# Two more Strassen pairs in block 0, and sums made by accumulating transfers

## The chip, the cores and the metric

The kernel runs on one core of a Trainium2 chip. The time is device time of one execution in microseconds; the median of three executions is given, and the profile is of one more execution. Engines are named as in the profile: PE (matrix products), DVE (vector), ACT (activation), POOL (GpSimd), SP (issues transfers). PE's weight loads are shown apart, as PEld.

## The reference

With x = A_u (2048 rows of 640) the result is x plus two branches that both start from a layer norm without scale:

```
xn = (x - mean) / sqrt(var + eps)                    # over the 640 columns
A  = causal convolution of xn with an S4D kernel, plus xn * D_skip
B  = mish(xn @ w1 + b1) @ w2                         # 640 -> 1728 -> 640
return x + A + B
```

Branch B is nearly all the arithmetic. mish(h) is h * tanh(softplus(h)).

## The kernel before

**Tiling.** The 2048 rows are worked in four blocks b of 512. Everything is held transposed: 640 features are five slabs k of 128 partitions, rows are the free dimension. F = 1728 is cut into 14 chunks f (thirteen of 128, and f = 8 of 64). Each fp32 product is three fp16 products (high x high, low x high, high x low), so the weights (W1H, W1L, W2H, W2L) and x (XH, XL) are split into high and low halves: ACT rounds the high half (`hi_w1` L522, `hi_w2` L529, `hi_x` L535), DVE makes the low half.

**A chunk.** The first layer (`mm1`, fifteen matmuls of 512 columns, L773) fills a PSUM bank, which the profile calls h or tr. The mish chain follows on ACT and DVE: sigmoid (L863), product with h (L867), three polynomial steps on ACT (L872, L877, L882), product (L887), rounding (L894) and low half (L905). The second layer (`mm2`, fifteen matmuls, L825) adds into five banks acc; it runs three chunks behind the first.

**Pairs by Strassen's identity.** In blocks 1 to 3 the first layers of the chunk pairs starting at 0, 2, 4, 6, 9, 11 are made together (`mm1_pair`, L775): 54 matmuls of 256 columns (L793) in five parts named one, two, three_a, three_b and four, in place of 60. It needs sums of weights of the two chunks (SWH, SWL, and the unused high half of W1H), sums of x (TH, TL, EH, EL), and between its parts two copies on ACT (cV L1029 and cY L1030, PSUM to a buffer and PSUM to PSUM) and two sums on DVE (z L1033, which part three_a waits for, and w L1037). Second-layer matmuls are woven between the parts. The sums of weights are made once, for block 1: SP loads both chunks again (`load_s`, two whole chunks a pair), DVE makes four sums (`sum_w`), then ACT and DVE round them (`hi_s` L568, `lo_s` L572). Block 0 has only plain chunks.

**The next block's x.** During block b, SP loads the rows of block b + 1 in four tiles for the statistics on DVE (L597 to L599) and the transposed x in five slabs (`load_xt`). POOL makes the inverse deviation (`rstds`), PE transposes mean and deviation into one bank (`spread` L608, after chunk 7 in block 0 and inside the pair at chunk 6 later), ACT copies it (L612), SP stores it to DRAM (sd, L616) and loads it back spread over all partitions (bc, L620, two tiles). DVE subtracts the mean and multiplies (`norm_t` L624, ten instructions a block). ACT and DVE split the result and make the sums of x (`sum_x`, `hi_t`, `lo_t`).

**The rest.** Branch A is reduced to two running sums per slab (`skip_a` to `skip_e`: DVE scans L715 and L719, the result L729 added into the slab xt). At a block's end the acc banks go to buffers r (`join`, L734 on DVE and L736 on ACT), and POOL's transfers do the rest: `add_x` (L518) adds the original x into r, `finish` (L739) adds r into xt, `store` (L742) writes xt out. The first two are accumulating transfers. SP also loads w1 and w2 again, transposed, for a check of their size (L666, L669).

**What sets the order.** The class `Plan` writes the program: each piece of work is added with its engine, a cost, what it needs (pre), the buffer it takes and, for transfers, kilobytes. PE's order is fixed by the code; every other engine takes, by these costs, the piece with the earliest due time among those ready. A transfer is taken to share one line with all others at 300 KB a microsecond, and to land 1.9 us after its bytes; `add_x` and `finish` are charged at twice their bytes, 512 for 256 KB. The result is a fixed order of instructions on each engine; at run time each engine works in that order and waits where it must. POOL and SP issue their transfers in order too. Semaphores of transfers are eight for each of the two queues, used in turn.

Of the kernel before, what the change touches and what calls it, by code (L numbers as in the profile page):

```python
# [20 lines left out]
P = 128  # L21
L = 2048
D = 640
# [10 lines left out]
HALF = 8  # L34
LAG = 3
# [201 lines left out]
def ffn_general(tc, x, xT, vec, w1, w2, out):  # L237
# [3 lines left out]
    with ExitStack() as es:  # L241
# [12 lines left out]
        for b in range(NB):  # L254
# [11 lines left out]
            for f, (n, o) in enumerate(zip(FC, FO)):  # L266
# [5 lines left out]
                for k in range(KD):  # L272
                    pe.matmul(h[:n], W1[:, k, :n], XN[:, k], start=k == 0, stop=k == KD - 1)
# [149 lines left out]
def body(ctx: ExitStack, tc: tile.TileContext, x, xT, logA, Aim, Cr, Ci, logdt, vec, w1, w1T, w2, w2T, out):  # L423
# [64 lines left out]
    XT, ACT, SM, NX = ({} for _ in range(4))  # L488
    NCHK = NF + 3 * KD
# [51 lines left out]
    def load_s(i, j):  # L541
# [3 lines left out]
    def sum_w(i, j):  # L545

        w = lambda n, m: kf(pl["sw", i, n])[:, 0:4].rearrange("p (q j) f -> p q j f", j=2)[:, :, m]
        t = lambda n: pl["ss", i, n // 2].rearrange("p (j q f) -> p j q f", j=2, q=2)[:, n % 2]
        if j == 0:
            v.tensor_tensor(t(0), w(1, 0), w(1, 1), op=OP.add)  # L550
        elif j == 1:
            v.tensor_tensor(t(1), t(0), w(0, 0), op=OP.subtract)
        elif j == 2:
            v.tensor_tensor(t(2), w(0, 0), w(1, 0), op=OP.subtract)
        else:
            v.tensor_tensor(t(3), w(0, 1), t(1), op=OP.subtract)

    def part_w(i, j):
        f = PAIRS[i] + 1
        t = pl["ss", i, j // 2].rearrange("p (j q f) -> p j q f", j=2, q=2)  # L560
        if j == 0:
            sh, sl = (w[f][:, 0:4].rearrange("p (q j) f -> p q j f", j=2)[:, :, 0] for w in (W1H, W1L))
            return sh, sl, t[:, 0]
        return (SWH[i][:, 0], SWL[i][:, 0], t[:, 1]) if j == 1 else (SWH[i][:, 1:3], SWL[i][:, 1:3], t)
# [12 lines left out]
    def sum_x(c, j):  # L577

        x = XT[c][:, 0:4].rearrange("p (q j) t -> p q j t", j=2)
        b11, b12, b21, b22 = (x[:, :, i, h] for i in range(2) for h in (CA, CB))  # L580
        p, q = ((b12, b11), (b22, j == 1 and stage(c, 0)), (b22, b12), (b21, j == 3 and stage(c, 1)),
                (XT[c][:, 4, CA], XT[c][:, 4, CB]))[j]
        v.tensor_tensor(stage(c, j), p, q, op=OP.subtract)

    def hi_t(c, j):
        a.activation(EH if j == 4 else TH[j], stage(c, j), AF.Copy, scale=SX)

    def lo_t(c, j):
        hi, lo = (EH, EL) if j == 4 else (TH[j], TL[j])
        v.scalar_tensor_tensor(lo, stage(c, j), SX, hi, op0=OP.mult, op1=OP.subtract)  # L590
# [27 lines left out]
    def spread_l(c):  # L618
        for j in range(2):
            sp.dma_start(pl["b", c][j], NX["sd"][j * NT:(j + 1) * NT].rearrange("(o i) p -> o (i p)", o=1).to_broadcast([P, TB]))  # L620

    def norm_t(c, k, j):
        z = XT[c][:, k]
        v.tensor_tensor(z, z, pl["b", c][j], op=(OP.subtract, OP.mult)[j])  # L624

# [118 lines left out]
    def bank(b, f):  # L744

        if b > 0:
# [3 lines left out]
    def mm1_part(f, kinds, c, start=False, stop=False, ks=range(KD)):  # L750
# [3 lines left out]
        for j, ((w, x), k) in enumerate(seq):  # L754
            pe.matmul(bank(0, f)[:, c], w[:, k], x[k][:, c], start=start and j == 0, stop=stop and j == len(seq) - 1)  # L755

    def mm1(b, f):
# [3 lines left out]
        hh, lh, hl = ([(h, w[f][:, k], x[k]) for k in range(KD)] for w, x in ((W1H, xh), (W1L, xh), (W1H, xl)))  # L761
# [13 lines left out]
    def mm1_pair(b, f):  # L775

        i = PAIRS.index(f)
        wh = [[W1H[f + j][:, k] for k in range(KD)] for j in range(2)]
        wl = [[W1L[f + j][:, k] for k in range(KD)] for j in range(2)]
# [133 lines left out]
    def whole():  # L913
# [8 lines left out]
        def chain(b, f, pre, drop=()):  # L922
# [7 lines left out]
            elif b > 0 and f in PAIRS:  # L930
# [52 lines left out]
        for f in range(3, NF):  # L983
            prev = {3: 0, 4: 1}.get(f, f - 2)
            add(("m1", 0, f), M, 15 * M5 if FC[f] == P else 1.85, mm1, 0, f,
                pre=[("hw1", f), ("ow1", f), ("v1", 0, prev), ("sg", 0, prev)] if f > 3 else [("v1", 0, prev), ("sg", 0, prev)])
            chain(0, f, [("m1", 0, f)])
            if f == 7:
                add(("spread", 1), M, 0.1, spread, pre=[("rs", 1)])
            for o in second(0, f - LAG, []):  # L990
                o()


        def vc(b):
            return ("vX", b - 1, PAIRS[-1]) if b > 1 else ("v1", 0, 2)

        for b in range(1, NB):
            for f in range(NF):
                n = (b, f)
                if f - 1 in PAIRS:  # L1000
# [3 lines left out]
                if f not in PAIRS:  # L1004
                    pb = before(b, f)
                    add(("m1", *n), M, 15 * M5 if FC[f] == P else 1.85, mm1, b, f,
                        pre=[("v1", b, f - 2), ("sg", b, f - 2)])
                    chain(b, f, [("m1", *n)])
                    for o in second(*g2, []):
# [3 lines left out]
                c = b  # L1013
                one, two, three_a, three_b, four = mm1_pair(b, f)
                p0 = (b, PAIRS[i - 1]) if i else (b - 1, PAIRS[-1])
                first = b == 1 and i == 0
                lastB = ("v1", 0, LAST) if first else ("v1", *before(b, f)) if f in (0, 9) else ("v1", *p0)
                lastC = ("v1", 0, LAST - 1) if first else ("v1", p0[0], p0[1] + 1)
                lastA = [("v1", 0, 2), ("sr", 1)] if first else [("cY", *p0), ("vX", *p0)]
                if (b, i) in ((1, 4), (2, 4), (3, 4)) and b < NB - 1:  # L1020
                    lastA.append(("sr", b + 1))
                if (b, i) == (NB - 1, NP - 1):
                    lastA.append(("oke",))
                SWD = lambda j: [("os", i, j)] if b == 1 else []
                TXD = lambda j: [("tl", b, j)]
                XLD = lambda ks: [("lo", b, k) for k in ks]
                A2, B2 = second(*g2, [9] if FC[g2[1]] == P else [6]), second(*h2, [3, 9] if FC[h2[1]] == P else [2, 6])
                add(("one", *n), M, 12 * M2, one, pre=lastA + SWD(0) + TXD(0) + XLD((0, 2)))
                add(("cV", *n), A, 0.36, lambda: a.copy(PVS, PV), pre=[("one", *n)] + ([] if first else [("w", *p0)]))  # L1029
                add(("cY", *n), A, 0.36, lambda: a.copy(PY, PX), pre=[("cV", *n), lastC])  # L1030
                A2[0]()
                add(("two", *n), M, 15 * M2, two, pre=[("cY", *n)] + SWD(1) + TXD(1) + XLD((1, 3, 4)))
                add(("z", *n), V, 0.38, lambda: v.tensor_tensor(PZ, PY, PVS, op=OP.add), pre=[("two", *n), lastB])  # L1033
# [7 lines left out]
                if i == NP - 2 and b == NB - 1:  # L1041
                    add(("oks",), M, 0.1, ok_sum, pre=[("ce", "last"), ("vX", *n)])
# [7 lines left out]
                chain(b, f + 1, [("four", *n), ("w", *n)])  # L1050

# [30 lines left out]
        for c in range(1, NB):  # L1082
            b = c - 1
            t0 = start(b, 0)
            for i in range(NT):
                add(("lx", c, i), S, 0.1, lambda c=c, i=i: sp.dma_start(pl["x", c, i], xr[c, i]),
                    pre=[("st", c, i - 2)] if i > 1 else [], take=("x", ("x", c, i), 1), rel=t0, kb=327.0)
# [4 lines left out]
            add(("bc", c), S, 0.2, spread_l, c, pre=[("sd", c)], take=("b", ("b", c), 2 * KD), kb=512.0)  # L1092
# [260 lines left out]
```

## Time and profile before

| | |
|---|---|
| time, three executions | 360.25, 360.0, 360.2 us; median 360.2 |
| the profiled execution | 359.29 us, of which the span of the core 357.5 us |
| bytes moved | 48.75 MB in 26036 packets, mean 136 GB/s |
| granted PE clock | 1.0 |
| POOL | 72 instructions, 50.4 us |

The span is what the profile's shares refer to; 1.79 us of the execution's own time lie outside it. In rows of a list of groups, `x15` is a count, the number before a comma is busy time, the one behind the mean in ns of one instruction. A row of the timeline has the start, the duration, the engine and line, and in brackets how long the engine stood idle before it and what the profile takes to have ended that. Rows on transfers give the kilobytes of one and the median time from its issue to its landing.

### The profile page before, as it was taken

The page shows a single profiled execution, that of the slowest core. Times are in us where ns is not written, and L with a number is a line of the kernel's source. Part 1 is how long each engine was busy: PE and PEld are TensorE (multiplying, and loading weights), DVE is VectorE, ACT ScalarE, POOL GpSimd, SP SyncE. Part 2 cuts the span into 40 slices and gives each one's busy share as a digit, 9 for nine tenths or more (in the row PEclk, how much of TensorE's full clock was granted, in tenths as well). Part 3 has the DMA queues.
Part 4 walks back from the last instruction along what each step waited for, and adds up shares of the span by engine and source line. Part 5 has one row for each costly group of instructions (what it writes and reads, how often), then busy time and mean ns, then how long its engine had stood idle before and what let it go on. Part 6 is the DMA issues. An engine that isn't in the chain of part 4 may idle for free.

```text
span 357.5 us, 6018 instructions
## 1 busy us (share of the span) xinstructions
PE 350.6 (98%) x2167; PEld 211.5 (59%) x2167; DVE 311.1 (87%) x585; ACT 296.3 (83%) x614; POOL 50.4 (14%) x72
## 2 busy tenths in 40 slices
PE   7999999999999999999999999999999999999995
PEld 6754444444666665665566666566566666566543
DVE  5989989989998999999999986899997888775552
ACT  3599999978488799889989897989978989868740
POOL 2100020000013041000103343000003552000000
PEclk9999999999999999999999999999999999999999
DMA  7879975105109954911256973941111994201003
GB/s 238 279 240 296 337 247 174 73 1 183 39 21 194 335 165 127 296 24 39 64 179 128 202 181 91 278 170 35 33 35 20 166 232 89 55 0 31 0 16 141
DMA packets 26036, 48.75 MB, mean 136 GB/s; under 512 B 3576, under 2 KB 6928, under 8 KB 26000
## 3 DMA queue, kind: packets, MB, share of 16 engines
q1 hardware_dynamic: 19152, 34.21, 29.8%
q0 software_dynamic: 6240, 13.11, 17.8%
q10 hardware_dynamic: 608, 0.98, 0.8%
q8 instruction: 19, 0.31, 0.4%
q14 instruction: 17, 0.14, 0.2%
HBM read 39.10 MB, written 5.26 MB: 124 GB/s over the span
## 4 chain that ended last, share of the span: by engine, by line
PE 95%; DMA 1%; DVE 1%; SPq 0%; ACT 0%; issue 0%; DVEq 0%
PE acc L825 48%; PE h L793 18%; PE h L773 14%; PE tr L793 12%; DMA x<-in_A_u_dram 1%; PE h L755 1%; PE tr L755 1%; PE acc L1217 0%; PE acc L839 0%; PE acc L836 0%; PE acc L837 0%; DVE w1l L526 0%; DVE st L598 0%; SPq L1236 0%; DVE st L597 0%
## 5 line engine op out<-in xcount | busy, mean ns | idle before, releaser
L825 PE MATMUL acc<-hi,w2h 128*128 128x512 f16 x273 | 100.9, 379 | 0.0
L825 PE MATMUL acc<-hi,w2l 128*128 128x512 f16 (+1 forms) x265 | 99.7, 379 | 0.0
L825 PE MATMUL acc<-lo,w2h 128*128 128x512 f16 x253 | 93.3, 379 | 0.0
L825 PEld LDWEIGHTS <-w2h 128*128 128x128 f16 x526 | 51.2, 98 | 48.4 <-issue 1.3
L863 ACT ACTIVATE s<-h,cv 128x512 f32<-128x512 f32 (+1 forms) x51 | 30.9, 605 | 23.6 <-PE h L793 18.4
L793 PEld LDWEIGHTS <-w1h 128*128 128x128 f16 x432 | 42.3, 98 | 10.7
L887 DVE SCALAR_TENSOR_TENSOR A<-p,A 128x512 f32<-128x512 f32 (+1 forms) x56 | 38.2, 682 | 7.2 <-ACT p L882 7.0
L825 PEld LDWEIGHTS <-w2l 128*128 128x128 f16 x273 | 25.6, 98 | 30.7 <-issue 1.1
L872 ACT ACTIVATE p<-s,kc 128x512 f32<-128x512 f32 (+1 forms) x56 | 40.1, 715 | 0.5
L882 ACT ACTIVATE p<-p,kc 128x512 f32<-128x512 f32 (+1 forms) x56 | 40.0, 714 | 0.2
L877 ACT ACTIVATE p<-p,kc 128x512 f32<-128x512 f32 (+1 forms) x56 | 39.9, 713 | 0.2
L905 DVE SCALAR_TENSOR_TENSOR lo<-A,hi 128x512 f16<-128x512 f32 x52 | 35.3, 680 | 3.6 <-ACT hi L894 3.3
L867 DVE SCALAR_TENSOR_TENSOR A<-h,bs,s 128x512 f32<-128x512 f32 (+1 forms) x51 | 33.0, 647 | 6.2 <-ACT s L863 6.0
L894 ACT ACTIVATE hi<-A 128x512 f16<-128x512 f32 (+1 forms) x56 | 34.9, 624 | 3.6 <-DVE A L887 3.4
L518 POOL DMA_DIRECT2D r<-in_xT_dram x15 | 13.7, 1094 | 126.8 <-ACT r L736 60.3
L773 PEld LDWEIGHTS <-w1h 128*128 128x128 f16 (+1 forms) x174 | 15.3, 99 | 20.3 <-issue 3.3
L715 DVE TENSOR_TENSOR_SCAN g<-g,car,kc 128x512 f32<-128x512 f32 x20 | 25.6, 1278 | 1.1 <-ACT g L709 1.1
L793 PEld LDWEIGHTS <-w1l 128*128 128x128 f16 x216 | 21.1, 98 | 8.4 <-issue 0.3
L719 DVE TENSOR_TENSOR_SCAN g<-g,car,g 128x512 f32<-128x512 f32 x20 | 25.5, 1276 | 0.1
L793 PE MATMUL tr<-xh,w1h 128*128 128x256 f16 x90 | 24.5, 273 | 0.1
L793 PE MATMUL tr<-xl,w1h 128*128 128x256 f16 x90 | 24.5, 273 | 0.0
L793 PE MATMUL tr<-xh,w1l 128*128 128x256 f16 x90 | 24.5, 273 | 0.0
(174 smaller groups left out, 728.7 us busy)
## 6 DMA issues: line engine op xcount, KB each, us to landing
w<-in_w_dram SPq DMA_DIRECT2D x23, 320.0 KB, 4.7
w<-in_w2T_dram SPq DMA_DIRECT2D x15, 288.0 KB, 6.4
w<-in_B_w_dram SPq DMA_DIRECT2D x13, 320.0 KB, 3.5
w<-in_w1T_dram SPq DMA_DIRECT2D x13, 320.0 KB, 6.6
x<-in_A_u_dram SPq DMA_DIRECT2D x12, 320.0 KB, 5.0
xt<-in_xT_dram SPq DMA_DIRECT2D x15, 256.0 KB, 5.5
r<-in_xT_dram POOLq DMA_DIRECT2D x15, 256.0 KB, 6.0
xt<-r POOLq DMA_DIRECT2D x15, 256.0 KB, 4.1
```

The costliest lines, as they stand in the source:

```text
L715: v.tensor_tensor_scan(g1[:, 1:], g1[:, 1:], zero.to_broadcast([P, TB]), car[:, 1, k:k + 1], op0=OP.add, op1=OP.add)
L773: pe.matmul(o, w, x, start=(j == 0), stop=(j == len(order) - 1))
L793: pe.matmul(o, p, q, start=start and n == 1, stop=n == 3 * len(w), skip_group_check=True)
L825: pe.matmul(o, w, x, start=start, stop=stop)
L863: a.activation(pl["s", b, f][:n, c], src(b, f) if h is None else h, AF.Sigmoid, bias=cv[:n, f:f + 1], scale=1 / SH)
L867: v.scalar_tensor_tensor(pl["A", b, f][:n, c], src(b, f) if h is None else h, bs[:n, f:f + 1], pl["s", b, f][:n, c], op0=OP.add, op1=OP.mult)
L872: a.activation(pl["p", b, f][:n], pl["s", b, f][:n], AF.Arctan, bias=one[:n], scale=-1.0)
L877: a.activation(p, p, AF.Square, bias=pi4[:n], scale=2.0)
L882: a.activation(p, p, AF.Tanh, bias=mb[:n], scale=MG)
L887: v.scalar_tensor_tensor(A, pl["p", b, f][:n], MC, A, op0=OP.add, op1=OP.mult)
L894: a.activation(hi[:n], A, AF.Copy, scale=MA * SA / SH)
L905: v.scalar_tensor_tensor(lo, A, MA * SA / SH, hi[:n], op0=OP.mult, op1=OP.subtract)
```

## The change

1. **Block 0.** With `EARLY = 4`, block 0 takes the pairs at chunks 9 and 11 by the identity too. Their sums of weights are made early, first of all pairs, and the sums of x of block 0 are made on DVE and ACT. `spread` of block 1 moves from behind chunk 7 to behind chunk 8.
2. **Sums of weights.** w1's slabs are stored in the order `KP`, so that the two slabs of a sum lie together. A pair gets one tile y of 512 KB: SP loads into it three pieces (256, 128 and 128 KB; the first is one piece of the second chunk written twice), POOL adds two accumulating transfers (384 KB: one piece of the second chunk added three times; then 128 KB of the first), and one DVE sum remains of four. Rounding is two ACT and two DVE instructions a pair, of 256 and 768 columns, in place of three each.
3. **x minus mean.** The subtraction on DVE is replaced by three accumulating POOL transfers a block (`center`: 512, 512 and 256 KB) which add the negated mean, spread from DRAM, to the slabs of xt. bc is one tile. DVE keeps the multiplication.
4. **Around it.** The identity's z is made with negated y, since the order of the sums is another; the statistics' rows share the buffers w; the skip sums, weight checks and mode sums get other due times.

The core of the diff:

```diff
+KP = (0, 2, 1, 3, 4)
...
+    EARLY = 4
+    paired = lambda b, f: f in PAIRS and (b > 0 or PAIRS.index(f) >= EARLY)
...
-    pl.pool("x", tiles(row, "x", 2, [P, D]))
-    pl.pool("t", tiles(row, "t", 4, [P, TB]))
+    pl.pool("t", tiles(row, "t", 3, [P, TB]))
+    pl.pool("y", tiles(row, "y", 2, [P, 4, 2, P]))
...
-    pl.pool("b", [[row.tile([P, TB], F32, name=f"bc{j}") for j in range(2)]])
+    pl.pool("b", tiles(row, "bc", 1, [P, TB]))
...
+    def parts(i, j, k):
         o = D * FO[PAIRS[i] + j]
-        sp.dma_start(kf(pl["sw", i, j]), w1[o:o + D * P].rearrange("(p k f) -> p k f", p=P, k=KD))
+        t = w1[o:o + D * P].rearrange("(p k f) -> p k f", p=P, k=KD)[:, 2 * k:2 * k + 2]
+        return t.rearrange("p k (o f) -> p o k f", o=1)
+
+    def load_s(i):
+        y = pl["y", i]
+        for j, k, at, m in ((1, 1, 0, 2), (0, 0, 2, 1), (0, 1, 3, 1)):
+            sp.dma_start(y[:, at:at + m], parts(i, j, k).to_broadcast([P, m, 2, P]))
+
+    def sum_w(i, n):
+        y = pl["y", i]
+        if n < 2:
+            j, m = ((1, 3), (0, 1))[n]
+            at = 0 if n == 0 else 1
+            g.dma_start(y[:, at:at + m], parts(i, j, 0).to_broadcast([P, m, 2, P]), accum_op=OP.add)
         else:
-            v.tensor_tensor(t(3), w(0, 1), t(1), op=OP.subtract)
+            v.tensor_tensor(y[:, 3], y[:, 3], y[:, 1], op=OP.add)
...
+    def center(c, n):
+        z = XT[c][:, 4:5] if n == 2 else XT[c][:, 0:4].rearrange("p (q j) t -> p q j t", j=2)[:, :, n]
+        m = NX["sd"][0:NT].rearrange("(o q i) p -> o q (i p)", o=1, q=1)
+        g.dma_start(z, m.to_broadcast([P, 1 if n == 2 else 2, TB]), accum_op=OP.add)
+
+    def norm_t(c, k):
         z = XT[c][:, k]
-        v.tensor_tensor(z, z, pl["b", c][j], op=(OP.subtract, OP.mult)[j])
+        v.tensor_tensor(z, z, pl["b", c], op=OP.mult)
...
+            for n in range(3):
+                add(("ce", c, n), G, 1.0, center, c, n, pre=[("lxt", c), ("sd", c)], kb=(512.0, 512.0, 256.0)[n])
             for k in range(KD):
-                add(("n", c, k, 0), V, 0.62, norm_t, c, k, 0, pre=[("lxt", c), ("bc", c)], drop=[("b", c)])
-                add(("n", c, k, 1), V, 0.62, norm_t, c, k, 1, pre=[("n", c, k, 0)], drop=[("b", c)])
+                add(("n", c, k, 1), V, 0.62, norm_t, c, k, pre=[("ce", c, 2 if k == 4 else k % 2), ("bc", c)], drop=[("b", c)])
...
+        order = [*range(EARLY, NP), *range(EARLY)]
         for i, f in enumerate(PAIRS):
+            early = i >= EARLY
+            add(("ls", i), S, 0.1, load_s, i, pre=[("os", order[order.index(i) - 2], 1)] if order.index(i) > 1 else [], take=("y", ("y", i), 2), rel=start(0, 3) if early else max(start(0, 8), start(1, f) - 40), kb=512.0)
+            for j in range(3):
+                add(("ss", i, j), V if j == 2 else G, 0.36 if j == 2 else 1.0, sum_w, i, j, pre=[("ss", i, j - 1) if j else ("ls", i)],
+                    kb=(384.0, 128.0, 0.0)[j])
```

**Where instructions stand.** Three places show how the order moves. Line numbers are those of the kernel that a row is from; behind the change they are L553 load_s, L560 sum_w, L571 hi_s, L628 center, L632 norm_t, L1024 cV, L1025 cY, L1028 z, L1032 w.

POOL, from the statistics of block 1 on, before (its fourth row begins the work at the end of block 0):

```order
L603 TENSOR_SCALAR st_row<-mv 128x4 [waits DVE_49]
L604 TENSOR_TENSOR st_row<-st_row,kc 128x4 [waits Pool_49]
L1193 COPY st_row<-mv 128x4
L518 DMA r_235<-in_xT_dram 128x512 [waits Activation_49]
L518 DMA r_236<-in_xT_dram 128x512 [waits DVE_49]
```

The same place on POOL now; the names y are the tiles of sums, in_w_dram is w1:

```order
L560 DMA y_230<-in_w_dram 128x3x256 [waits DMAHW1_49,DMAHW0_49]
L560 DMA y_231<-in_w_dram 128x3x256 [waits DMAHW5_49,DMAHW4_49]
L560 DMA y_230<-in_w_dram 128x256 [waits DMASW0_49]
L560 DMA y_231<-in_w_dram 128x256 [waits DMASW1_49]
L606 TENSOR_SCALAR st_row<-mv 128x4 [waits DVE_49]
L607 TENSOR_TENSOR st_row<-st_row,kc 128x4 [waits Pool_49]
L1191 TENSOR_SCALAR st_row<-mv 128x4
L628 DMA xt<-sd 128x2x512 [waits DMAHW7_49,DMAHW5_49,DMAHW2_49]
L628 DMA xt<-sd 128x2x512 [waits DMAHW6_49,DMAHW0_49]
L560 DMA y_230<-in_w_dram 128x3x256 [waits DMAHW3_49,DMAHW4_49,DMASW2_49,DVE_49]
L628 DMA xt<-sd 128x512 [waits DMAHW1_49]
L560 DMA y_230<-in_w_dram 128x256 [waits DMASW6_49]
```

The four early sums stand ahead of the statistics of block 1, the centrings behind them, and the first sum of pair 0 behind two of the three centrings.

ACT around the first rounded sum of pair 0, before (in block 0, w1h_114 is the high half that block 1 needs):

```order
L877 ACTIVATE p_247<-p_247,kc 64x512 [waits Activation_49]
L568 ACTIVATE w1h_114<-t_229 128x2x128 [waits DVE_49]
L882 ACTIVATE p_247<-p_247,kc 64x512 [waits Activation_49]
L529 ACTIVATE w2h_152<-w_223 128x640 [waits DMAHW3_49]
L863 ACTIVATE s_243<-h_211,cv 128x512 [waits PE_49]
```

And now, in block 0's second pair (chunk 11):

```order
L879 ACTIVATE p_246<-s_241,kc 128x512 [waits Activation_49]
L571 ACTIVATE w1h_114<-y_230 128x256 [waits DMAHW3_49,DMASW6_49]
L870 ACTIVATE s_240<-h_212,cv 128x512 [waits DVE_49,PE_49]
L884 ACTIVATE p_246<-p_246,kc 128x512 [waits Activation_49]
L879 ACTIVATE p_245<-s_240,kc 128x512 [waits Activation_49]
L889 ACTIVATE p_246<-p_246,kc 128x512 [waits Activation_49]
L1024 COPY pvs<-tr 128x256 [waits PE_49]
L1025 ACTIVATE h_212<-tr 128x256 [waits DVE_49]
```

The rounding waited for DVE, and waits now for a transfer of POOL (DMASW6); cV and cY of the pair stand six rows behind it.

DVE around z of the pair at chunk 9 in block 1, before:

```order
L624 TENSOR_TENSOR xt<-xt,bc_240 128x512 [waits DMAHW7_49,DMAHW3_49]
L572 SCALAR_TENSOR_TENSOR w1l_138<-t_232,w1h_125 128x2x128 [waits Activation_49]
L887 SCALAR_TENSOR_TENSOR A_245<-p_247,A_245 64x512 [waits Activation_49]
L1033 TENSOR_TENSOR h_211<-h_212,pvs 128x256 [waits PE_49]
L624 TENSOR_TENSOR xt<-xt,bc_240 128x512 [waits DMAHW0_49]
```

And now:

```order
L736 SCALAR_TENSOR_TENSOR xt<-xt,cc,g_233 128x512 [waits DVE_49]
L632 TENSOR_TENSOR xt<-xt,bc_239 128x512 [waits DMAHW7_49,DMAHW0_49,DMASW5_49]
L632 TENSOR_TENSOR xt<-xt,bc_239 128x512 [waits DMAHW1_49,DMASW6_49]
L632 TENSOR_TENSOR xt<-xt,bc_239 128x512 [waits DMAHW2_49]
L1028 SCALAR_TENSOR_TENSOR h_211<-h_212,pvs 128x256 [waits PE_49,Activation_49]
```

One subtraction stood ahead of z, which waited for SP's transfers; now three multiplications stand there, which wait for the first two centrings (DMASW5, DMASW6). In block 2 all five stand ahead of z of the pair at chunk 9, the last waiting for the third centring.

More of the change, by code (lines that the diff above doesn't have):

```diff
@@ L982, in whole @@
             chain(0, f, [("m1", 0, f)])
[L983 to L998, printed above, removed]
+        used = {0: ("v1", 0, 0), 1: ("v1", 0, 1)}
+        p0 = None
+        for b in range(NB):
+            for f in range(0 if b else 3, NF):
                 n = (b, f)
-                if f - 1 in PAIRS:
+                if paired(b, f - 1):
                     continue
@@ L1030, in whole @@
-                add(("cY", *n), A, 0.36, lambda: a.copy(PY, PX), pre=[("cV", *n), lastC])
+                own = [("ow1", f + j) for j in range(2) if f > 3] if b == 0 else []
+                add(("one", *n), M, 12 * M2, one, pre=lastA + SWD(0) + TXD(0) + XLD((0, 2)) + own)
+                add(("cV", *n), A, 0.36, lambda: a.copy(PVS, PV), pre=[("one", *n)] + ([("w", *p0)] if p0 else []))
+                add(("cY", *n), A, 0.36, lambda: a.activation(PY, PX, AF.Copy, scale=-1.0), pre=[("cV", *n), used[1]])
@@ L1148, in whole @@
             add(("kc", c, k), V, 1.2, skip_c, c, k, pre=[("kb", c, k)])
-            late = [("lo", c, k)] + ([("tx", c, i) for i in range(4)] if k < 4 else [("tx", c, 4)]) if c else []
+            late = ([("lo", c, k)] if c else []) + ([] if EARLY == NP and c == 0 else [("tx", c, i) for i in range(4)] if k < 4 else [("tx", c, 4)])
             add(("ke", c, k), V, 0.66, skip_e, c, k, pre=[("kc", c, k)] + late, drop=[("g", c, k)], due=due)
```

111 lines of the change are left out of this document (44 added, 67 removed).

## The prediction

> **What bounds the kernel now.** I read the page's shares first, then the waits of PE, then the chain that ended last.
>
> ```profile
> span 357.5 us, 6018 instructions
> PE 350.6 (98%) x2167; PEld 211.5 (59%) x2167; DVE 311.1 (87%) x585; ACT 296.3 (83%) x614; POOL 50.4 (14%) x72
> q1 hardware_dynamic: 19152, 34.21, 29.8%
> q0 software_dynamic: 6240, 13.11, 17.8%
> ```
> ```profile
> PE tr L1231 <- POOL car L464: 1.4, 1, 1.4
> PE acc L1217 <- DVE x L1201: 0.6, 2, 0.3
> ```
> ```profile
> 53.79 1.29 PE h L773 x8
> 55.09 3.24 PE acc L825 x15
> 58.32 3.24 PE h L773 x15
> ...
> 90.71 1.94 PE acc L825 x9
> ...
> 103.08 1.94 PE acc L825 x9
> ...
> 150.91 1.97 PE h L793 x18
> ...
> 235.72 1.97 PE h L793 x18
> ```
>
> PE works 98% of the span, and its two largest groups of waits come to 2.0 us. The chain is PE matmuls almost throughout (the third fence, start and length of each piece). So only fewer matmuls, or a new wait of PE, can change the time; a wait that costs PE nothing today has at most some microseconds of cover, and that cover is what has to be counted.
>
> **The gain.** A plain chunk costs one first and one second layer, 3.24 us each (55.09 to 58.32, and the step after it), so two cost 12.95 us. A pair by the identity repeats from 90.71 to 103.08, 12.37 us. The change puts two more pairs into block 0: 2 x 0.58 = 1.16 us less of PE. That is the whole gain on the bound engine. The subtractions that DVE loses (15 of 0.68 us and 18 sums of weights) are no gain by themselves, since PE does not wait for DVE. ACT gets the early sums' rounding, the conversions of x and the copies of two pairs in a stretch where it is full:
>
> ```profile
> 20.00:40.00 20.00, 20.00 (x94) 9.06 (x93) 18.57 (x36) 20.00 (x35) 0.00 (x0) 1.00 0.92 300
> 40.00:60.00 20.00, 20.00 (x97) 8.98 (x96) 18.82 (x43) 19.91 (x32) 2.17 (x3) 1.00 0.71 220
> 60.00:80.00 20.00, 20.00 (x96) 8.78 (x94) 19.47 (x33) 17.97 (x40) 0.00 (x0) 1.00 0.20 72
> ```
>
> (Columns: PE, PEld, DVE, ACT, POOL busy, granted clock, DMA share, GB/s.) I cost that ACT and DVE work at nothing: it is hidden by the lead with which weights are converted ahead of their chunks and by the 2.0 us that ACT has free from 60 to 80. If that cover is gone, PE loses a few tenths to 2 us.
>
> The early sums also move transfers ahead of block 0's own weights: two times 512 KB on SP's queue and as much accumulated on POOL's. The hardware queue's share, 29.8% of 357.5 us for 34.21 MB, is 3.1 us a megabyte, the software queue's 17.8% for 13.11 MB is 4.85: together 8.3 us of transfer time. From 20 to 60 us the engines have 1.6 + 5.8 = 7.4 us free, so the weights behind them come at most about 1 us later on balance, which I also cost at nothing; the price if their lead is gone stands with rival 3.
>
> **What a transfer of GpSimd costs.** POOL's queue gets nine centrings and twelve sums (SP loads 18 pieces for them in place of 12, and three broadcasts in place of six). The nearest rows:
>
> ```profile
> r<-in_xT_dram POOLq DMA_DIRECT2D x15, 256.0 KB, 6.0
> xt<-r POOLq DMA_DIRECT2D x15, 256.0 KB, 4.1
> xt<-in_xT_dram POOLq DMA_DIRECT2D x5, 256.0 KB, 3.7
> ```
> ```profile
> 105.99 2.90 POOL L518 DMA_DIRECT2D r<-in_xT_dram  x3 [58.98 <-ACT r L736]
> 111.80 0.89 POOL L518 DMA_DIRECT2D r<-in_xT_dram  x1 [2.92 <-ACT s L863]
> ...
> 141.72 0.86 POOL L739 DMA_DIRECT2D xt<-r  x1 [5.80 <-DVE xt L729]
> 150.16 0.58 POOL L742 DMA_DIRECT2D out_dram<-xt  x1 [7.57 <-DMA xt<-r]
> ...
> 190.84 2.69 POOL L518 DMA_DIRECT2D r<-in_xT_dram  x3 [15.31 <-DVE r L734]
> 196.47 0.88 POOL L518 DMA_DIRECT2D r<-in_xT_dram  x1 [2.95 <-ACT s L863]
> ```
> ```profile
> 107.34 1.25 ACT L736 ACTIVATE r<-acc 128x512 f32<-128x512 f32 x2 [0.80 <-PE acc L825]
> ```
>
> The first group gives 3.7 us for 256 KB where little else runs. Each further 256 KB is about 1.3 us at 4.85 us a megabyte: a 512 KB centring takes 5.0 us, a sum of 384 KB 4.3 us. Beside SP's loads it is dearer: the accumulation issued at 141.72 held the store that waits for it until 150.16, over 8 us for 256 KB.
>
> The second group shows more. Three accumulations of 256 KB go out back to back at 105.99; the fourth goes out at 111.80 although its own input, the second join of the ACT row, was done at 107.34 + 1.25 = 108.59. It left 5.8 us after the first, about the time a transfer takes to land; at 190.84 and 196.47 the same. So GpSimd's queue holds three of 128 rows each and no fourth. A centring of 512 KB has 256 rows, the first sum of a pair 384. Two such do not fit beside each other if it is rows that count, and each then starts when the one before has landed. I take that as the likelier reading, since the only other cause named, an ACT sigmoid, is no input of that transfer. The written order leaves little room for it: its costs charge a finish of 256 KB as 512 KB, but a centring of 512 KB as 512, so the work behind a centring is placed as if it moved at twice a finish's pace.
>
> The Trainium skill, in "DMA: Bandwidth & Descriptors", section "Anatomy of one DMA — SWDGE (gpsimd) path", fits such a transfer by about 2.0 us and the bytes at 436 GB/s. An estimate by that page is 3.2 us for a centring, well under what I use; the rows of this trace are longer already at half its size, so the trace does not agree.
>
> **(a) The second pair of block 0.** ACT rounds the first summed weights of pair 0, needed in block 1 only, just ahead of the sigmoid and the copies of the pair at chunk 11; the sums stand on POOL behind two centrings. These start from the mean's chain:
>
> ```profile
> 54.11 0.35 SPq L616 DMA_DIRECT2D sd<-sr  x1
> 56.69 1.12 SPq L620 DMA_DIRECT2D bc<-sd  x2
> ```
> ```profile
> L863 ACT ACTIVATE s<-h,cv 128x512 f32<-128x512 f32 (+1 forms) x51 | 30.9, 605 | 23.6 <-PE h L793 18.4
> L882 ACT ACTIVATE p<-p,kc 128x512 f32<-128x512 f32 (+1 forms) x56 | 40.0, 714 | 0.2
> L1029 ACT COPY pvs<-tr 128x256 f32<-128x256 f32 x18 | 6.6, 369 | 4.9 <-PE tr L793 4.5
> L1030 ACT COPY h<-tr 128x256 f32<-128x256 f32 x18 | 6.8, 376 | 0.0
> L568 ACT ACTIVATE w1h<-t 128x256 f16<-128x256 f32 x6 | 2.4, 405 | 0.0
> ```
>
> The transposition of the mean now follows chunk 8, at 55.09 (it stood after chunk 7); a quarter of a microsecond each for it and its copy puts the mean's store at 55.7, and 2.58 us later (54.11 to 56.69) the first centring may go, 58.3. One after the other: 58.3 + 5.0 = 63.3, 63.6 + 5.0 = 68.6, and with 0.3 us to start, the sum 68.9 + 4.3 = 73.2. Slightly dearer under what is left of SP's loads, I take 73.6. Behind the rounding on ACT come a sigmoid, three polynomial steps and the two copies: 0.405 + 0.605 + 3 x 0.714 + 0.369 + 0.376 = 3.9 us, so PE gets its input at 77.5. It wants it at 58.32 + 12.37 + 1.31 + 1.94 = 73.94. The wait is 3.6 us. If both centrings take 8 us it is up to 9, and it is nothing if the three transfers can overlap, since the sum then lands before 70.
>
> **(b) Block 1, pair at chunk 9.** Three multiplications by the standard deviation's inverse stand on DVE ahead of the pair's sum z; the second of them waits for the second centring of block 2, and PE's third part waits for z.
>
> ```profile
> 137.11 0.29 SPq L616 DMA_DIRECT2D sd<-sr  x1
> 138.34 0.82 SPq L620 DMA_DIRECT2D bc<-sd  x2
> 139.21 2.57 SPq L666 DMA_DIRECT2D w<-in_w1T_dram  x5
> ```
> ```profile
> L624 DVE TENSOR_TENSOR xt<-xt,bc 128x512 f32<-128x512 f32 x30 | 19.7, 681 | 0.0
> L1033 DVE TENSOR_TENSOR h<-h,pvs 128x256 f32<-128x256 f32 x18 | 7.7, 428 | 6.5 <-PE h L793 6.3
> ```
>
> I count from the mean's store. PE's third part begins 150.91 - 137.11 = 13.8 us after it, and up to 1.1 us later if the store waits less, as it does in block 3 (below). The centring may go 1.23 us after the store, and stands behind one finish (0.86): 2.1. SP's loads start at that time, so the first takes the 8.1 us of such company, the second 6.4, between that and 5.0: 2.1 + 8.1 + 0.3 + 6.4 = 16.9. Two multiplications and z are 1.8 us: 18.7, a wait of 3.8 to 4.9, taken as 4.4. Ends: 0.4 with 5.0 each, 6.6 with 8.1 each.
>
> **(c) Block 2, pair at chunk 9.** Here z stands behind the multiplication of the last slab, so behind all three centrings, and one finish stands between them.
>
> ```profile
> 220.79 0.29 SPq L616 DMA_DIRECT2D sd<-sr  x1
> 222.18 0.80 SPq L620 DMA_DIRECT2D bc<-sd  x2
> ```
>
> PE's third part begins 235.72 - 220.79 = 14.9 us after the store; the centrings 1.4 us after it: 1.4 + 8.1 + 0.3 + 6.4 + 0.3 + 4.1 (the 256 KB median) + 1.1 = 21.7, a wait of 6.8. Ends: 1.9 with quiet transfers, 12 if all take 8.1.
>
> **The sum**: -1.16 + 3.6 + 4.4 + 6.8 = +13.6 us. The profiled run took 359.29, a span of 357.5 and 1.8 around it, 0.25% under the median of 360.2; by the median it becomes 373.8, say 374. Half a microsecond here and there, where POOL's stores stand behind a centring, is left to the range.
>
> **The rivals.**
> 1. GpSimd's transfers overlap after all (the gap before the fourth had another cause). Then (a) vanishes. (b) and (c) are bounded by bytes: 1.31 MB of centring at 4.85 us is 6.4 us beside about ten SP loads of 320 KB, at 3.1 us a megabyte 10 us. Interleaved, the last centring lands some 16 us after its start: (c) about 4.5, (b), needing two of three, about 1.7. Sum +5, 365 us.
> 2. The centrings overlap and SP's loads do not slow them, so each lands inside its cover. It decides at the second centring of block 2 landing within 13.8 - 1.8 = 12.0 us of the mean's store, and the last of block 3 within 14.9 - 1.1 = 13.8. Both together, after 2.1 us, are 3.7 - 1.3 = 2.4 us of latency and 1.05 MB at 4.85 us, 5.1: 9.6 us, so it can be. Then only the 1.16 us remain: 359.0, faster by 0.3%. The 8 us at 141.72 and the 6.0 us median at 256 KB speak against it. By the fit of the Trainium skill named above, with 3.2 us a centring even one after the other, this would be the time; the rows, longer at half the size, leave it little.
> 3. Transfers of 1 KB rows cost as much a row as ones of 2 KB. The four early sums then take twice as long; they stand on POOL ahead of the variance of block 1, and the transposition of the mean in PE's own order waits for that. Each of the four at the 8 us of the contended row, in turn from the middle twenties, where SP's order puts their loads, ends near 57; the variance's steps on POOL then put the transposition at about 60, 5 us late, and 3 us more go where the weights of block 0 queue behind: 382. No row shows 1 KB accumulations, so it has a small chance.
>
> **How the numbers follow.** The likeliest, 58%, is 374. Rival 1 has 22%, rival 2 9%, rival 3 8%, and 3% remain for transfers that end so close that it looks like no change. The range holds the first, third and forecast cases and their ends: from 363 (rival 1 with (b) at 0) to 386 (all at 8 us). About 0.2%, 0.7 us, is what a measurement of this kernel tells from no change. Faster 0.09, same 0.03, slower 0.88.
>
> **What would show it.** In the waits of PE of the changed kernel: part two of the pair at chunk 11 waiting on ACT's copy for 3 to 4 us near 74; the third part of the pairs at 9 in blocks 1 and 2 waiting on DVE's z. On POOL, consecutive centrings starting 5 to 8 us apart, each at the landing of the one before. Centrings 1.8 us apart would show rival 1; PE without waits and a span near 356.4, rival 2; a wait at the mean's transposition near 55, rival 3. I am wrong if DVE's or ACT's queue has other work that PE needs ahead of these, or if a wait sits where the order shows none of this.

## The result and the profile after

The changed kernel takes 401.34 us (median of 6; 398.23 to 402.33) against 360.0 us: a ratio of 1.1138 (95% interval 1.1096 to 1.118), 41 us slower. I had said 374, in a range of 363 to 386. The direction, the places and the order of the transfers held; the size did not, and one cost was missing from the sum.

The page of the changed kernel (busy time of PE; queue, kind, packets, MB, share of 16 engines) and PE's waits (total, times, longest):

```profile
span 399.7 us, 6187 instructions
PE 357.7 (89%) x2215; PEld 219.0 (55%) x2215; DVE 302.9 (76%) x562; ACT 300.0 (75%) x619; POOL 72.8 (18%) x93
...
q0 software_dynamic: 11568, 20.19, 27.3%
q1 hardware_dynamic: 20352, 32.64, 25.5%
```
```profile
PE tr L800 <- ACT h L1025: 17.2, 3, 9.3
PE h L800 <- DVE h L1028: 16.6, 3, 10.4
PE tr L1229 <- POOL car L465: 1.5, 1, 1.5
```

The span grew by 42.2 us in the profiled execution. Two new groups of waits make 17.2 + 16.6 = 33.8 us: PE's second part waits for ACT's copy cY, its third part for DVE's z. Another 7.1 us is PE's own busy time, 357.7 against 350.6, although it has less to do. DVE is less busy than before (302.9 against 311.1), and that gained nothing.

GpSimd's transfers, from the timeline of POOL (start, duration, idle before it and what ended that):

```profile
58.10 1.28 POOL L628 DMA_DIRECT2D xt<-sd  x1 [6.68 <-DMA sd<-sr]
66.38 1.22 POOL L628 DMA_DIRECT2D xt<-sd  x1 [7.00 <-issue]
74.05 1.28 POOL L560 DMA_DIRECT2D y<-in_w_dram  x1 [6.45 <-issue]
...
154.00 1.56 POOL L628 DMA_DIRECT2D xt<-sd  x1
168.17 2.15 POOL L628 DMA_DIRECT2D xt<-sd  x2 [12.61 <-issue]
...
249.80 1.24 POOL L628 DMA_DIRECT2D xt<-sd  x1 [3.25 <-issue]
262.42 1.21 POOL L628 DMA_DIRECT2D xt<-sd  x1 [11.39 <-issue]
...
268.95 0.86 POOL L628 DMA_DIRECT2D xt<-sd  x1 [4.40 <-issue]
```

The large ones go one at a time, as forecast, but the next transfer follows them only 8.3 and 7.7 us later in block 0, and 14.2 and 12.6 us later for the first centring in blocks 1 and 2. The next two fences are the transfers of 249.8 to 262.4 and of 262.4 to 269 (KB of each, median us to landing):

```profile
w<-in_w2T_dram SPq DMA_DIRECT2D x8, 288.0 KB, 8.9
xt<-sd POOLq DMA_DIRECT2D x1, 512.0 KB, 12.3
```
```profile
xt<-sd POOLq DMA_DIRECT2D x1, 512.0 KB, 6.2
```

Beside eight loads of SP the centring takes 12.3 us, beside the last one 6.2.

What that does, on DVE and ACT at the second and third place, and on PE's chain:

```profile
174.38 1.29 DVE L632 TENSOR_TENSOR xt<-xt,bc 128x512 f32<-128x512 f32 x2 [5.82 <-DMA xt<-sd]
175.59 0.43 DVE L1028 SCALAR_TENSOR_TENSOR h<-h,pvs 128x256 f32<-128x256 f32 x1
...
262.27 1.29 DVE L632 TENSOR_TENSOR xt<-xt,bc 128x512 f32<-128x512 f32 x2 [7.61 <-DMA w<-in_w2T_dram]
```
```profile
263.00 0.63 ACT L538 ACTIVATE xh<-xt 128x512 f16<-128x512 f32 x1 [7.24 <-DVE xt L632]
...
264.53 0.38 ACT L1025 ACTIVATE h<-tr 128x256 f32<-128x256 f32 x1
```
```profile
88.19 1.97 PE h L800 x18
...
176.06 3.97 PE h L800 x18
```
```profile
88.00:90.00 2.00, 2.00 (x20) 1.76 (x19) 1.02 (x3) 0.94 (x2) 0.00 (x0) 1.00 0.90 143
...
175.00:178.00 3.00, 1.94 (x10) 1.34 (x10) 3.00 (x6) 0.20 (x1) 0.52 (x1) 0.50 0.69 161
```

z stands right behind the multiplications that waited for the centring (175.59). In block 2 there is a second path: ACT's conversion of the first slab (L538) waits for its multiplication, and cV and cY of the pair stand behind it, so PE waits twice there (5.9 and 4.7 us). The last two fences show the rest (the second is of stretches of time: start:end, length, busy PE, PEld, DVE, ACT and POOL, granted clock, DMA share, GB/s): eighteen matmuls of the same part take 1.97 us at a granted clock of 1.00, and 3.97 right after a wait, where it is 0.50.

### The profile page after: what moved, and what is told of

It is laid out like the page before. It is cut to its first block, busy times and chain, and to the rows that moved or that the text cites. A ratio compares the mean times of both kernels' runs of the same rounds, so it can differ in the third digit from the quotient of the medians.

```text
span 399.7 us, 6187 instructions
## 1 busy us (share of the span) xinstructions
PE 357.7 (89%) x2215; PEld 219.0 (55%) x2215; DVE 302.9 (76%) x562; ACT 300.0 (75%) x619; POOL 72.8 (18%) x93
## 4 chain that ended last, share of the span: by engine, by line
PE 55%; issue 18%; ACT 10%; DMA 8%; DVE 5%; POOL 3%; ACTq 0%; POOLq 0%; DVEq 0%
PE acc L832 27%; PE h L800 15%; PE tr L800 8%; PE h L780 4%; DMA xt<-sd 3%; DMA w<-in_A_u_dram 2%; DMA y<-in_w_dram 2%; ACT s L870 1%; DMA w<-in_w_dram 1%; ACT w1h L525 1%; ACT p L889 1%; ACT p L884 1%; ACT p L879 1%; POOL r L521 1%; POOL xt L628 1%
## 5 line engine op out<-in xcount | busy, mean ns | idle before, releaser
L800 PEld LDWEIGHTS <-w1h 128*128 128x128 f16 x480 | 47.9, 100 | 12.8
L800 PE MATMUL tr<-xh,w1h 128*128 128x256 f16 x100 | 28.0, 280 | 17.2 <-ACT h L1025 17.2
L800 PEld LDWEIGHTS <-w1l 128*128 128x128 f16 x240 | 23.9, 100 | 27.3 <-issue 18.1
L800 PE MATMUL h<-th,swh 128*128 128x256 f16 x80 | 22.8, 285 | 16.6 <-DVE h L1028 16.6
L632 DVE TENSOR_TENSOR xt<-xt,bc 128x512 f32<-128x512 f32 x15 | 10.0, 688 | 25.8 <-DMA xt<-sd 18.2
L800 PE MATMUL tr<-xh,w1l 128*128 128x256 f16 x100 | 28.1, 281 | 0.0
L800 PE MATMUL tr<-xl,w1h 128*128 128x256 f16 x100 | 28.1, 281 | 0.0
L800 PEld LDWEIGHTS <-swh 128*128 128x128 f16 x240 | 24.5, 102 | 6.0 <-issue 0.2
L746 POOL DMA_DIRECT2D xt<-r x15 | 13.6, 908 | 75.1 <-DVE xt L736 40.0
```

Of the source, the lines that this page charges most:

```text
L746: g.dma_start(XT[b][:, k], pl["r", b, k], accum_op=OP.add)
L800: pe.matmul(o, p, q, start=start and n == 1, stop=n == 3 * len(w), skip_group_check=True)
```

## The experiments

All figures are medians against runs of the kernel before on the same chip (359.8 to 360.0); brackets hold the ratio and its 95% interval.

**Descriptor room.** The builder's option for GpSimd's descriptors was 1024 bytes a partition.

```diff
-_BACC = {"dynamic_dma_scratch_size": 1024}
+_BACC = {"dynamic_dma_scratch_size": 2048}
```

> The changed kernel with twice the room for GpSimd's transfer descriptors (2048 instead of 1024 bytes a partition), nothing else. Theory 1, the queue's room lets big transfers go only one at a time: the second centring starts some 2 us after the first instead of at its landing, the wait at chunk 11 of block 0 (9.3 us) goes, the two in blocks 1 and 2 (10.4 and 10.6 us) halve, and the clock recovers with them: about 375 us. Theory 2, the transfers are slow by themselves beside SP's loads and share one rate: starting earlier brings little, 395 us or more.

384.2 us, ratio 1.0672 (1.0619 to 1.0725). On POOL and in PE's waits:

```profile
57.88 2.52 POOL L628 DMA_DIRECT2D xt<-sd  x2 [6.32 <-DMA sd<-sr]
...
145.30 3.74 POOL L628 DMA_DIRECT2D xt<-sd  x3
...
238.68 2.45 POOL L628 DMA_DIRECT2D xt<-sd  x2 [3.08 <-issue]
```
```profile
PE tr L800 <- ACT h L1025: 10.4, 3, 4.9
PE h L800 <- DVE h L1028: 8.1, 1, 8.1
```

The centrings now go out back to back, three of them at 145.30, so the room was what held them one by one. That is worth 17 us, and 18.5 us of waits remain: theory 1 holds for some two fifths of the loss, and theory 2 has a share. The 375 us of theory 1 were not reached.

**Company of SP's loads.** The same order of instructions, with the loads for the check of w1 and w2 cut to 16 columns. ACT squares only these 16, and the check is left out.

```diff
-            sp.dma_start(t[:FC[j]], w1T[FO[j]:FO[j] + FC[j]])
+            sp.dma_start(t[:FC[j], 0:16], w1T[FO[j]:FO[j] + FC[j], 0:16])
...
-            sp.dma_start(t[:, 0:F // 3], w2T[k * P:(k + 1) * P, i * F // 3:(i + 1) * F // 3])
+            sp.dma_start(t[:, 0:16], w2T[k * P:(k + 1) * P, i * F // 3:i * F // 3 + 16])
```

> The changed kernel in the same order of instructions, where the loads of w1 and w2 for the check of their size take 16 columns of a row instead of 640 or 576, and the check's outcome is not used: it leaves out that check. SP's traffic beside the centrings of blocks 1 and 2 is gone, the descriptor room is as in the change. If company with SP makes the centrings of 12 to 14 us, they fall to about 6, the waits of 10.4 and 10.6 us at chunk 9 to about 2 and 3, and the time to some 382. If the descriptor room alone makes them, nothing changes: 400.

> The same with 2048 bytes for descriptors. With neither company nor one transfer at a time, all three waits for centrings should go and what is left is the wait at chunk 11 of block 0 and the one near 110: 366 to 370 us. If it stays above 375, a third cause is missing.

388.3 us (1.0787; 1.0713 to 1.0861) with the small room, 369.2 (1.0278; 1.0236 to 1.0321) with the larger. The POOL timeline of the first:

```profile
151.10 1.57 POOL L628 DMA_DIRECT2D xt<-sd  x1
160.78 2.15 POOL L628 DMA_DIRECT2D xt<-sd  x2 [8.11 <-issue]
...
244.03 1.24 POOL L628 DMA_DIRECT2D xt<-sd  x1 [3.20 <-DMA w<-in_w2T_dram]
250.69 1.21 POOL L628 DMA_DIRECT2D xt<-sd  x1 [5.42 <-issue]
```

From the first centring in block 1 to the next it is 9.7 us instead of 14.2; it still runs beside a finish and loads of rows. In block 2, where the checks' loads were nearly all that ran beside it, it is 6.7 instead of 12.6: there company makes the difference. The waits at chunk 9 shrink less than expected, to 6.5 and 5.7 us, and the time is 388 instead of 382. Of the 41 us, room alone gives back 17, company alone 13, both 32: the two roughly add up, and neither explains the loss by itself. A part of the 13 may come from ACT, which has 13 us less work in this run (286.7 against 300.0); no run separates that.

**What a wait of PE costs.** In the kernel before, z of one pair is computed n times over:

```diff
-                add(("z", *n), V, 0.38, lambda: v.tensor_tensor(PZ, PY, PVS, op=OP.add), pre=[("two", *n), lastB])
+                add(("z", *n), V, 0.38, lambda b=b, i=i: [v.tensor_tensor(PZ, PY, PVS, op=OP.add) for _ in range(1 + 12 * ((b, i) == (1, 4)))], pre=[("two", *n), lastB])
```

(30 in place of 12 for the long one.)

> The kernel before, with the pair's sum z at chunk 9 of block 1 computed 13 times instead of once on DVE (the same values again), so that PE's third part waits. Twelve sums of 0.43 us are 5.1 us, of which some 1.5 us are covered: a wait of about 3.6 us. If a wait costs only its length, 363 to 364 us and no more busy time of PE than before (350.6). If PE's clock falls in such a wait, PE's busy time grows by some 2 us.

> The same with 31 sums: 12.9 us, a wait of about 11.4 us, like the longest of the changed kernel. If a wait costs only its length, 371 to 372 us with PE busy 350.6. If the clock falls in the wait and recovers only after some microseconds of work, PE's busy time grows by 2 to 3 us, and the time is 374.

366.5 us (1.0183; 1.0159 to 1.0207) and 374.2 us (1.0398; 1.0374 to 1.0421). Of the short one PE's wait, its busy time and stretches of 2 us:

```profile
PE h L793 <- DVE h L1033: 4.2, 1, 4.2
```
```profile
PE 353.6 (97%) x2167; PEld 212.6 (58%) x2167; DVE 316.4 (87%) x597; ACT 296.5 (81%) x614; POOL 50.6 (14%) x72
```
```profile
150.00:152.00 2.00, 0.77 (x4) 0.26 (x3) 1.86 (x5) 1.99 (x6) 0.58 (x1) 1.00 0.49 197
152.00:154.00 2.00, 0.00 (x0) 0.00 (x0) 1.83 (x5) 0.86 (x3) 0.00 (x0) 0.90 0.02 8
154.00:156.00 2.00, 1.04 (x6) 0.72 (x6) 1.96 (x5) 0.00 (x0) 0.00 (x0) 0.50 0.04 8
156.00:158.00 2.00, 2.00 (x11) 1.40 (x10) 1.94 (x5) 0.00 (x0) 0.00 (x0) 0.50 0.00 0
...
160.00:162.00 2.00, 2.00 (x14) 1.32 (x13) 1.97 (x3) 0.94 (x3) 0.00 (x0) 0.89 0.00 0
162.00:164.00 2.00, 2.00 (x15) 1.25 (x13) 1.21 (x2) 1.93 (x5) 0.00 (x0) 1.00 0.00 0
```

A wait of 4.2 us drops the granted clock to 0.50, and it is back only some 5.5 us after PE restarts near 155: 3.0 us more of busy time (353.6 against 350.6), and a time 6.7 us longer for a wait of 4.2. The wait of 12.6 us costs 2.1 us more of busy time, with the clock back 3.9 us after the restart. The shortest wait that dropped the clock is one of 3.6 us, in block 0 of the run with the larger room (0.50 from 78 to 80); one of 3.3 us, in block 0 of the run with the larger room and the light checks, left it at 1.00. So a wait of 3.6 us or more costs its length and some 2 to 3 us. The Trainium skill states the rule in "TensorE: Matmul & The Clock Gate", Part 1: half rate after an idle window of about 3.4 us, full rate after as much busy time. The trace agrees in kind, and not in each length: in both made waits the clock fell some 2.8 us after the last matmul (an estimate from the granted clock of the stretches from 150 to 154), and it took 3.9 and 5.5 us to come back.

**Parts of the change alone.** Subtraction back on DVE (the mean in a row buffer, `center` gone):

```diff
-            for n in range(3):
-                add(("ce", c, n), G, 1.0, center, c, n, pre=[("lxt", c), ("sd", c)], kb=(512.0, 512.0, 256.0)[n])
...
+                add(("n", c, k, 0), V, 0.62, norm_t, c, k, 0, pre=[("lxt", c), ("bm", c)], drop=[("m", c)])
```

> The changed kernel with the subtraction of the mean back on DVE (the mean loaded by SP into one of the shared row buffers), sums of weights still by GpSimd. If the centrings are what PE waits for, directly or because the sums stand behind them, the waits at chunk 9 of blocks 1 and 2 vanish and the one at chunk 11 of block 0 too: 360 to 364 us. If the sums are as dear by themselves, over 375.

374.4 us (1.0387; 1.0344 to 1.0431). Without centrings 27 us come back and the three waits are gone. The 360 to 364 expected did not come. PE's largest wait, then POOL and ACT ahead of it:

```profile
PE tr L803 <- ACT h L1028: 7.1, 3, 6.5
```
```profile
108.18 0.87 POOL L521 DMA_DIRECT2D r<-in_xT_dram  x1 [6.41 <-ACT r L746]
109.24 0.86 POOL L521 DMA_DIRECT2D r<-in_xT_dram  x1 [0.19 <-issue]
118.21 1.30 POOL L560 DMA_DIRECT2D y<-in_w_dram  x1 [8.12 <-issue]
```
```profile
123.40 0.42 ACT L571 ACTIVATE w1h<-y 128x256 f16<-128x256 f32 x1 [7.27 <-DMA y<-in_w_dram]
```

A sum of 384 rows stands behind two transfers of 128 rows and goes out 9 us later; ACT's rounding waits for it, and cV and cY of the pair stand behind that: place (a) again, one block later, and without a centring. Sums back on DVE instead, centrings kept:

```diff
-            g.dma_start(y[:, at:at + m], parts(i, j, 0).to_broadcast([P, m, 2, P]), accum_op=OP.add)
...
+            v.tensor_tensor(y[:, 0], w(1, 0), w(1, 1), op=OP.add)
```

> The changed kernel with the sums of weights made by DVE from whole chunks loaded by SP, as before the change; the centrings stay on GpSimd. If the centrings are the cause of the waits at chunk 9, these 21 us and the slow clock behind them stay, and only the waits at chunk 11 of block 0 and near 130 us go: 383 to 390 us. If the sums fill the queue and so delay the centrings, all shrink: under 375.

390.9 us (1.0874; 1.0804 to 1.0944). PE's largest waits:

```profile
PE h L802 <- DVE h L1034: 9.3, 3, 7.5
PE h L802 <- DVE h L1030: 5.2, 2, 4.7
PE acc L834 <- ACT r L745: 5.1, 1, 5.1
```

The waits of 21 us at chunk 9 did not stay as they were. In block 1 z now stands ahead of the multiplications, and the pair's other sum w (L1034) waits behind one, 7.5 us; in block 2 z waits 4.7 us. The rest lies at other places, 5.1 us of it at a copy of the acc banks at the end of a block. Both back on DVE, so that the pairs of block 0 alone remain:

> Only the first part of the change: block 0 takes its last two pairs by the identity, sums of weights and x minus mean on DVE. My sum for this part alone was -1.16 us: 358.9 against 360.0. If ACT or DVE in block 0 cannot take the added work, or block 0's weights come late, it is slower than before, 361 to 366.

373.4 us (1.0384; 1.035 to 1.0418), where I had 358.9. The first matmul of block 1 in the kernel before and in this one (two fences):

```profile
89.24 0.27 PE L793 MATMUL tr<-th,w1h 128*128 128x256 f16 x1
```
```profile
88.08 0.27 PE L805 MATMUL tr<-th,w1h 128*128 128x256 f16 x1
```

1.16 us earlier: the gain of block 0 is there. It is lost behind it. DVE has 318.2 us of work instead of 311.1; 2.1 us go at the first pair of block 1, some 3 in between, 6.9 near the end, where the scans of branch A come last on DVE (a wait of 4.5 us and the slow clock), and 2.9 behind the last matmul. Since the change had moved the due times of those scans, I put the old ones back:

```diff
-        edge = [start(1, 6), start(2, 2), start(3, 0), start(3, 11), start(3, 13)]
+        edge = [start(1, 4), start(2, 0), start(2, 11), start(3, 5), start(3, 11)]
```

> Only the two pairs in block 0, DVE doing all sums and the subtraction, and the due times of the skip sums and of the checks as they were before the change. The run with the change's due times lost 4.5 us to a wait for DVE at the end of the last block and in all 9 us to waits. If those due times did it, this one is at 359 to 362; if the added work of block 0 did it, it stays near 373.

372.8 us (1.0347; 1.0314 to 1.038): the due times are not it. The wait at the end shrinks and others of about 1 us appear from 97 to 140. Whether the added work of block 0 makes this loss is not shown: no run has all sums on DVE and no pair in block 0.

Side by side: the pairs alone take 373.4 us; with the sums on GpSimd added it is 374.4, with the centrings added instead 390.9, and with both 401.3. So the centrings cost 17.5 us beside sums on DVE and 27 beside sums on GpSimd, and the sums on GpSimd cost 1 us without centrings and 10.5 with them. Each of these orders was written anew, so the differences hold for these orders alone.

**The order.** The same transfers as in the change; only the costs from which the order is written are those that the profile shows.

```diff
-                add(("ce", c, n), G, 1.0, center, c, n, pre=[("lxt", c), ("sd", c)], kb=(512.0, 512.0, 256.0)[n])
+                add(("ce", c, n), G, (8.0, 8.0, 5.0)[n], center, c, n, pre=[("lxt", c), ("sd", c)], kb=(512.0, 512.0, 256.0)[n])
...
-                add(("ss", i, j), V if j == 2 else G, 0.36 if j == 2 else 1.0, sum_w, i, j, pre=[("ss", i, j - 1) if j else ("ls", i)],
+                add(("ss", i, j), V if j == 2 else G, (5.5, 5.0, 0.36)[j], sum_w, i, j, pre=[("ss", i, j - 1) if j else ("ls", i)],
```

> The changed kernel with the same transfers, but the order written with the times that the profile shows for GpSimd's transfers (8, 8 and 5 us for the centrings and 5.5 and 5 for the sums, in turn) instead of 1 us and shared bytes. If PE's waits come from an order that expects the data too early, the multiplications move behind z and the waits of 34 us shrink to under 15: 370 to 380 us. If the transfers are simply too slow for the block, the waits move to other rows and the time stays near 400.

365.0 us (1.0139; 1.0117 to 1.0161). 36 of the 41 us are gone, more than I had expected. PE's largest group of waits, POOL and DVE:

```profile
PE tr L800 <- ACT h L1025: 1.7, 4, 0.6
```
```profile
141.04 1.47 POOL L628 DMA_DIRECT2D xt<-sd  x1
153.67 1.20 POOL L628 DMA_DIRECT2D xt<-sd  x1 [3.51 <-issue]
```
```profile
150.75 0.43 DVE L1028 SCALAR_TENSOR_TENSOR h<-h,pvs 128x256 f32<-128x256 f32 x1 [0.90 <-PE h L800]
153.36 0.69 DVE L632 TENSOR_TENSOR xt<-xt,bc 128x512 f32<-128x512 f32 x1 [1.20 <-DMA xt<-sd]
```

The centring is nearly as slow as before, 12.6 us to the next. But z now stands ahead of the multiplication that waits for it, and PE does not see it. Most of the loss came not from slow transfers as such, but from an order that expects them early. And 365.0 is 8 us under the 373.4 of the pairs with all that work on DVE. So in these orders the transfers make the pairs possible at less cost than DVE does, and still leave the kernel slower than before.

**What is left.** Four more runs with that order: without pairs in block 0, with one pair, with the subtraction on DVE, and with the larger room.

```diff
-    EARLY = 4
+    EARLY = 6
```

> The order written with the measured times of GpSimd's transfers, and no pair in block 0 (EARLY = 6): the transfers' part of the change alone. The run with both pairs and this order took 365.0, with 2.6 us lost by the start of block 1 where ACT had the added work. If that work is what remains, this one is at 361 to 362 (no gain of 1.16, no loss of block 0); if it is the transfers, it stays at 365.

> The same with one pair in block 0 (EARLY = 5). Half the gain, 0.58 us, and half of ACT's added work: 360 to 363 if ACT's work in block 0 is the limit; no different from two pairs, 365, if it is not.

> The subtraction of the mean on DVE, both pairs in block 0, and the sums of weights on GpSimd with their measured times (5.5 and 5 us) in the planned order. Without the measured times it took 374.4, with 6.7 us of wait for a sum near 126. If the planned time of the sums did that, 363 to 367; if the lack of room on DVE did, 372 or more.

> The order written with the measured times, both pairs, and twice the room for descriptors. If the order already covers the transfers, more room changes nothing: 364 to 366. If late transfers still cost what is left, 360 to 362.

365.3 (1.0141; 1.0124 to 1.0158), 366.2 (1.0165; 1.0131 to 1.0199), 372.7 (1.0338; 1.0307 to 1.0368) and 364.6 us (1.0143; 1.0114 to 1.0172). The pairs are not what keeps the planned order above the kernel before: none, one and two give the same within 1.2 us. More room changes nothing either. The subtraction on DVE is worse here, by the 372 us expected for a lack of room on DVE; but that cause is not shown, since PE's longest wait is the old one: 6.2 us near 125, for ACT's copy behind the rounding of a sum that went out 8 us after two transfers of 128 rows. One more run has the larger room and the old due times:

> The order written with the measured times and the larger room (364.6), and the due times of the skip sums and the checks as before the change. That one was 0.5 us ahead of the kernel before until block 2, and lost it in the last block. If its due times did that, 359 to 361; if DVE's and ACT's load did it, no change.

366.8 us (1.0196; 1.015 to 1.0243): those are not it either. None of the thirteen variants of the change beats the kernel before. The best lies 4.6 us above it (3.5 by the span of its profiled execution): 1.9 us of that are behind the last matmul, the rest is many waits below 1 us in changing places. Which decision of the order makes them stays open.

## Why the prediction was wrong

- **The gain**, 1.16 us: right, at the start of block 1 of the run with the pairs alone. That it fits to the hundredth is luck, since PE's waits ahead of that point differ by 0.2 us between the two runs.
- **One large transfer at a time**: right; the larger room lets three go together.
- **The places (a), (b) and (c)**: right. In (c) I missed that ACT's conversion also stands ahead of cV and cY, so the wait comes in two pieces.
- **The landing of a centring**: the step that failed, as the term "the first takes the 8.1 us of such company, the second 6.4", and "5.0" twice in (a). The 8.1 us belonged to 256 KB; I used it for 512 KB. Measured: 14.2 and 6.2 us in block 1, 12.6 and 6.5 in block 2, 8.3 and 7.7 in block 0, where I had counted on a quiet machine although the loads of the sums ran beside. That the 6.4 came out is luck: it was meant as a price half way to company, and 6.2 us is what a centring took with hardly any load of SP beside it, where I had 5.0. So (a) was 9.3 us instead of 3.6, (b) 10.4 instead of 4.4, (c) 5.9 + 4.7 instead of 6.8. The estimate of 3.2 us from the fit in the Trainium skill, "DMA: Bandwidth & Descriptors", section "Anatomy of one DMA — SWDGE (gpsimd) path", was further off still: the quietest centring of 512 KB took 6.2.
- **The clock**: not in the sum at all. PE's busy time should have fallen by 1.16 us and grew by 7.1; that is 8.3 us for four waits of 4.7 us and more, 2 us each, about what the two runs with a made wait show (3.0 and 2.1).
- **Small waits**, "left to the range": 2.1 and 1.6 us near 130, where sums of weights stand behind other transfers.
- **Together**: of the 27.5 us between 373.8 and 401.3, the three waits give 15.5 (30.3 instead of 14.8), the clock 8.3 and the small waits 3.7. The range ended at 386 because it took "all at 8 us" as the worst, by the same reading of a transfer of half the size, and had no clock.
- **"I cost that ACT and DVE work at nothing"**: left open. In the planned order it held: none, one and two pairs take 365.3, 366.2 and 365.0 us. The run with the pairs alone lost 13 us, but no run shows that block 0's work is what it lost them to.
- **The rivals**: the larger room makes the transfers overlap, as in rival 1, and gave 384, not 365; with the loads of the checks gone as well it gave 369. Of rival 2, 359 by transfers inside their cover, nothing came. Rival 3 did not come: no wait at the transposition of the mean.

## What to carry to other kernels

A duration read from a transfer holds for its size, its company and its place in the queue: here a centring of 512 KB beside SP's loads took 12 to 14 us where 256 KB had taken 8, and 6.2 us where 256 KB had taken 3.7 with little else running. So scale by bytes when the new transfer is larger. Where the order on each engine is fixed beforehand, the costs it was written with are part of the kernel: correcting five numbers gave back 36 of 41 us without moving a byte less. And a wait of PE of some 3.6 us or more is to be charged 2 to 3 us on top, for the clock.

## What the runs showed of the hardware

The room for GpSimd's descriptors is set by an option of the kernel's builder, and 1024 bytes a partition held three transfers of 128 rows, or one of 256 and one of 128 (168.17). Two of 256 rows never overlapped; with 2048 bytes two (57.88) and three centrings (145.30) went out back to back.

GpSimd's accumulating transfers fared badly beside SP's plain loads: in the changed kernel, from 154.1 to 168.2, SP's queue moved 2.87 MB in 1287 packets and GpSimd's 0.79 MB in 416. Why the latter got a quarter of the packets, and whether accumulating or the few transfers that its room admits make it so, was not settled. And more room shifted waiting from POOL into the transfers themselves: the nine centrings land after a median of 13.8 us with 2048 bytes against 7.1 with 1024.
